# First batch's low rank in two column groups, and the load queue in written order

## The chip, the cores and the metric

The kernel runs on one core of a Trainium2 chip. The metric is the device time of one execution in microseconds, the median over several runs. All stage times below are from one profiled execution of the kernel, counted from the start of its span.

The engines are named as the profile names them: PE is TensorE (PEld its weight loads), DVE is VectorE, ACT is ScalarE, POOL is GpSimd, and SP is SyncE, whose queue issues all the loads and stores of this kernel.

## The reference, cut to what matters

There are 4 batches, 8 heads, a sequence of 768 and a head dimension of 48. A gated recurrence is followed by a mixer with a low-rank mix along the sequence and two dense layers:

```python
f = 1.0 / (1.0 + np.exp(-f_logit))
for t in range(S):
    state = f[:, :, t, :, None] * state + np.einsum('bhd,bhe->bhde', k[:, :, t], v[:, :, t])
    y[:, :, t] = np.einsum('bhd,bhde->bhe', q[:, :, t], state)
x = y.transpose(0, 2, 1, 3).reshape(B, S, H * D)       # (4, 768, 384)
xt = x.transpose(0, 2, 1)
h = xt @ U @ V                                         # U (768, 32), V (32, 768)
u = x + h.transpose(0, 2, 1)
ch = np.maximum(u @ w_ch1, 0.0) @ w_ch2                # (384, 1536), (1536, 384)
return u + ch
```

All of it is 32-bit floating point inside the kernel; the mixer's weights arrive as 64-bit floats.

## The kernel before, in words

**Units.** The recurrence is done for two heads at a time. Such a pair is a *unit*, and a batch has four (`HP`), so there are 16. Unit n loads f, k and q into one of two sets of buffers (`late` for even n, `other` for odd) and v into `v_nat`. `front(n, ...)` makes the gates (`fz`), their running products (scans on DVE) and the scaled keys and queries. `rear(n, ...)` makes the chunk states (`kept`, `states`, `scan`), the scores (`scores`, with the masked product `A` on DVE), and the output in two parts that add up in one PSUM tile `y`: `read` (queries by states) and `inner` (`A` by v). `inner` ends with ACT's copy of `y` into the unit's 96 of the 384 columns of the batch's `x`. After `read`, ACT makes a tiny copy named `seen`.

**The mixer of a batch.** `low_rank` multiplies U by the six row blocks of x into four groups of 32 rows (`ph`), ACT copies the result to `h`; `added_up` adds the four groups with the matrix `blocks` (again `ph` and `h`); `mix` multiplies by V (`pu`) and DVE adds the result to x. `turn` transposes two row blocks of x (`put`), and ACT copies them to `uT`. `ch1` makes the first dense layer from `uT` and w1 (`pz`: six matmuls a call), and ACT evicts it with a ReLU to `z_all` or `zw`. `ch2` makes the second one (`po`). `pz` and `po` share a PSUM pool of two buffers; `pt`, `put`, `pu`, `y` and others share another of three.

**Weights.** `weight_loader` gives each piece of a weight a `start` (the DMA of the 64-bit words into a raw buffer) and an `end`: two passes on ACT (L90, L91), three on DVE (L92 to L94) and one on POOL (L95). The pieces are U, two of V, twelve column blocks of w1 (128 columns each, numbered 0 to 11 here) and twelve row blocks of w2. The first six blocks of w1 are loaded into halves of the buffers of `zw`, which are free until then; the others into `w_raw`, which has four buffers. `ahead_by` starts a load some pieces before the end of an earlier one.

**Order.** PE's order is written out by hand everywhere, that of DVE and ACT in the first batch's attention and what follows it up to `start_mixer(1, ...)`. SP's order is left to a scheduler. `busy(n)` issues n matmuls of no use (`idle`). The first batch's four units run alone, with little else for PE. Then its mixer starts: low rank, sum, part of x, transposes, with two single `busy` calls between, and then the `pz` groups, beside which the next batch's units are worked from the fourth `pz` on (`EARLY`).

**Loads.** The scheduler puts the loads of units 2 and 3, U, V and blocks 0 and 1 of w1, unit 4, most of unit 5, blocks 2 and 3, the v of unit 5, blocks 4 and 5, and then blocks 6 to 9 in SP's queue, in this order.

Of the kernel before, what the change touches and what calls it, by code (L numbers as in the profile page):

```python
# [10 lines left out]
F32 = mybir.dt.float32  # L11
U32 = mybir.dt.uint32
U64 = mybir.dt.uint64
I32 = mybir.dt.int32
AF = mybir.ActivationFunctionType
ALU = mybir.AluOpType
AX = mybir.AxisListType

WP = 384

RAW = 4
# [80 lines left out]
def ahead_by(n, loads):  # L102


    def call(i):
        if i + n < len(loads):
            loads[i + n][0]()
        loads[i][1]()

    return [lambda i=i: call(i) for i in range(len(loads))]  # L110
# [36 lines left out]
class Mixer:  # L147
# [6 lines left out]
    def __init__(self, tc, b, x, U, V, w1, w2, sums, ident, blocks, out, two, three, zp, ps_big, ps_mm, wide=False,  # L154
                 z_all=None, room=None, pair=0):
        nc = tc.nc
        P = nc.NUM_PARTITIONS
        NCH, DM = x.shape[1], x.shape[2]
        R, FF = U.shape[2], w1.shape[2]
        NG = P // R  # L160
        NDC, NFC = DM // P, FF // P
# [3 lines left out]
        uT, z, h, S = {}, {}, {}, {}  # L165

        def low_rank():
            pm = ps_mm.tile([P, 512], F32, name="ph", tag="mm")

            for c in range(NCH):  # L170
                g = slice((c % NG) * R, (c % NG + 1) * R)
                nc.tensor.matmul(pm[g, 0:DM], lhsT=U[:, c, :], rhs=x[:, c, :],  # L172
                                 start=(c < NG), stop=(c >= NCH - NG))
            h[0] = two.tile([P, DM], F32, name="h", bufs=1)
            nc.scalar.copy(h[0], pm[:, 0:DM])

        def added_up():

            pm = ps_mm.tile([P, 512], F32, name="ph", tag="mm")
            nc.tensor.matmul(pm[:, 0:DM], lhsT=blocks, rhs=h[0], start=True, stop=True)  # L180
            h[1] = two.tile([P, DM], F32, name="h", bufs=1)
            nc.scalar.copy(h[1], pm[:, 0:DM])

        def add(*args):

            with tc.high_priority(offset=AHEAD):
                nc.vector.tensor_tensor(*args)  # L187

        pu = {}

        def mix(t):

            s = t % 2
            if s == 0:
                pu[0] = ps_big.tile([P, 2, 512], F32, name="pu", tag="big")
            g = slice((t % NG) * R, (t % NG + 1) * R)
            nc.tensor.matmul(pu[0][:, s, 0:DM], lhsT=V[g, t // NG, :], rhs=h[1][g, :], start=True, stop=True)  # L197
            if s == 1:
                add(x[:, t - 1 : t + 1, :], x[:, t - 1 : t + 1, :], pu[0][:, :, 0:DM], ALU.add)

        def turn(a):

# [231 lines left out]
def factored_path(ctx, tc, q, k, v, f_logit, moe_U, moe_V, moe_w_ch1, moe_w_ch2, out, ok):  # L434
# [4 lines left out]
    nc = tc.nc  # L439
    B, H, S, D = q.shape  # L440
    P = nc.NUM_PARTITIONS
    C = P // 2
    NCH = S // C

    NBL = S // P
    HP = H // 2
    DM = H * D
    R = moe_U.shape[1]
    FF = moe_w_ch1.shape[1]
    NDC = DM // P  # L450
    NFC = FF // P
# [15 lines left out]
    two = ctx.enter_context(tc.tile_pool(name="two", bufs=2))  # L467
    three = ctx.enter_context(tc.tile_pool(name="three", bufs=3))
    zp = ctx.enter_context(tc.tile_pool(name="zp", bufs=3))
    ps_big = ctx.enter_context(tc.tile_pool(name="ps_big", bufs=3, space=bass.MemoryType.PSUM))  # L470
# [20 lines left out]
    def load(n, *names):  # L491

        b, hp = divmod(n, HP)
        for nm in names:
            if nm == "v":
                v_tiles[n] = three.tile([P, NBL, 2, D], F32, name="v_nat")
            for par in range(2):
                head = src[nm][b, 2 * hp + par]
                if nm == "v" and par:

                    for s in range(2):
                        nc.sync.dma_start(
                            out=v_tiles[n][(1 - s) * C : (2 - s) * C, :, par, :],
                            in_=head.rearrange("(c s p) d -> s p c d", s=2, p=C)[s],
                        )
                    continue
                if nm == "v" or n < TURNED:
                    dst = v_tiles[n] if nm == "v" else nat[n % 2][nm]
                    nc.sync.dma_start(out=dst[:, :, par, 0:D], in_=head.rearrange("(c p) d -> p c d", p=P))
                    continue  # L510
                head = head.rearrange("(c i) d -> i c d", i=NB)
                for part in range(2):
                    p0 = par * PAD + part * NB
                    n_ch = min(NB, D - part * NB)
                    nc.sync.dma_start(
                        out=raw[n % 2][nm][p0 : p0 + NB, :].rearrange("p (c d) -> p c d", d=NB)[:, :, 0:n_ch],
                        in_=head[:, :, part * NB : part * NB + n_ch],
                    )
# [9 lines left out]
    blocks = const.tile([P, P], F32, name="blocks")  # L528
# [33 lines left out]
    table = one.tile([P, 1], F32, name="table")  # L562
# [4 lines left out]
    U = const.tile([P, NBL, R], F32, name="U")  # L567
    V = const.tile([P, (NBL * R + P - 1) // P, P], F32, name="V")
    take_in = weight_loader(nc, two, nc.sync)
    weights = [take_in(U, moe_U.rearrange("(c p) r -> p c r", p=P))]  # L570
    weights += [take_in(*pair) for pair in by_rows(V, moe_V, R)]
    early = len(weights)
    w1_rows = moe_w_ch1.rearrange("(c p) f -> p c f", p=P)

    spare = []

    def place():
        if not spare:
            t = zp.tile([P, NFC // 2, 2 * P], F32, name="zw").rearrange("p i t -> p (i t)").bitcast(U64)
            spare.extend([t[:, 0:WP], t[:, WP : 2 * WP]])  # L580
        return spare.pop(0)

    FIRST = 6
    weights += [
        take_in(w1[:, :, i * P : (i + 1) * P], w1_rows[:, :, i * P : (i + 1) * P], place if i < FIRST else None)
        for i in range(NFC)
# [96 lines left out]
    def mixer(b):  # L683
        return Mixer(tc, b, x_tiles[b], U, V, w1, w2, sums if b else None, ident, blocks, out, two, three, zp, ps_big, ps_mm,
                     b == 0, z_all, room if b >= B - 2 else None, FEWER - (b - B + 2) * NCH // 4)
# [172 lines left out]
    def front(n, *names):  # L858

        if n >= NU:  # L860
            return []
        if n not in ahead:
            ahead[n] = dict(zip(("gates", "keep", "keys", "read_back", "queries"), prepare(n)))
        return [ahead[n].pop(nm) for nm in names]

    def rear(n, *names):

        if not 0 <= n < NU:
            return []
        if n not in here:  # L870
            here[n] = dict(zip(("kept", "states", "scan", "scores", "read", "inner"), attend(n)))
        return [here[n].pop(nm) for nm in names if nm in here[n]]
# [43 lines left out]
    with tc.manual_schedule(engines={nc.vector.engine, nc.scalar.engine}):  # L916


        idle = ps_mm.tile([P, 512], F32, name="idle", tag="mm")

        def busy(n):
            for _ in range(n):
                nc.tensor.matmul(idle[:, 0:DM], lhsT=ident, rhs=ends[:, 0:DM], start=True, stop=True)  # L923

        busy(1)
        for piece in front(0, "gates"):
            piece()
        for n in range(HP):
            pieces = front(n, "keep", "keys") + rear(n - 1, "scan", "scores")
            pieces += [lambda: busy(3)] + rear(n, "kept") + front(n, "read_back", "queries")  # L930
            if n + 1 < HP:
                pieces += front(n + 1, "gates") + rear(n - 1, "read", "inner") + rear(n, "states")
            else:
                pieces += rear(n, "states") + rear(n - 1, "read") + rear(n, "scan", "scores") + rear(n - 1, "inner")
            for piece in pieces:
                piece()
            if n < 2:
                load(n + 2, "v")
            if n == 1:


                for start, _ in weights[: early + 2]:
                    start()
            elif n > 1:
                load(n + 2, "f", "k", "q", "v")
        for start, _ in weights[early + 2 : early + FIRST]:
            start()
        loads = ahead_by(early + FIRST, weights)
        for piece in rear(HP - 1, "read") + loads[:2] + rear(HP - 1, "inner") + loads[2 : early + 1]:
            piece()  # L950
        loads = loads[early + 1 :]

        m = mixer(0)
        start = m.before[:5] + m.firsts[0:1] + m.before[5:]
        idles = {1: 1, 2: 1}

        EARLY = 9
        second = chain(front(HP, "gates", "keep", "keys", "read_back", "queries"), steps(HP, 2 * HP + 1))
        for i, (_, piece) in enumerate(start + m.firsts[1:]):
            busy(idles.get(i, 0))  # L960
            piece()
            if loads and i != 1:
                loads.pop(0)()
            if i >= EARLY:
                next(second)()
        for f in loads:
            f()
        n = len(m.seconds) // (NBL // 2)
        todo, after = m.seconds[:-n], m.seconds[-n:]

        attention(second, 12 + 10 * HP - (len(start) + len(m.firsts) - 1 - EARLY), todo)
        m = start_mixer(1, after)
        for f in to_sum:
            f()
# [380 lines left out]
```

## Time and profile before

| What | Value |
|---|---|
| Median of 14 runs | 490.84 us (487.68 to 492.75) |
| The profiled execution: its own time | 491.83 us |
| The profiled execution: its span | 490.1 us |
| Mean granted TensorE clock in it | 0.986 of full |
| Busy: PE, DVE, ACT, POOL | 472.8, 356.2, 163.6, 36.3 us |
| First `ph` matmul of the first batch | 49.18 us |
| First `pz` matmul | 58.61 us |
| Bytes moved by DMA | 34.34 MB |

A line of the timeline gives the start in us, the length in us, the engine, the line of the kernel and operation, the output and input tile, shapes, and the number of records; in brackets the idle time of the engine ahead of it and what ended it. One matmul of 32-bit floats leaves two records on PE. "issue" is time in which the engine waited for nothing that the profile shows. The line of 40 digits named PEclk gives the granted TensorE clock in tenths for each fortieth of the span. For SP the timeline shows when a DMA is issued, not when it lands.

### The profile page before, as it was taken

The page shows a single profiled execution, that of the slowest core. Times are in us where ns is not written, and L with a number is a line of the kernel's source. Part 1 is how long each engine was busy: PE and PEld are TensorE (multiplying, and loading weights), DVE is VectorE, ACT ScalarE, POOL GpSimd, SP SyncE. Part 2 cuts the span into 40 slices and gives each one's busy share as a digit, 9 for nine tenths or more (in the row PEclk, how much of TensorE's full clock was granted, in tenths as well). Part 3 has the DMA queues.
Part 4 walks back from the last instruction along what each step waited for, and adds up shares of the span by engine and source line. Part 5 has one row for each costly group of instructions (what it writes and reads, how often), then busy time and mean ns, then how long its engine had stood idle before and what let it go on. Part 6 is the DMA issues. An engine that isn't in the chain of part 4 may idle for free.

```text
span 490.1 us, 12681 instructions
## 1 busy us (share of the span) xinstructions
PE 472.8 (96%) x5519; PEld 402.1 (82%) x5519; DVE 356.2 (73%) x561; ACT 163.6 (33%) x307; POOL 36.3 (7%) x49
## 2 busy tenths in 40 slices
PE   7897999999999999999999999998999999999995
PEld 4676588886666568899899888898979999999995
DVE  5877798788998847656857548796896796948642
ACT  3343575654334313423231403433131312112200
POOL 3000245452000000000000000000000000000000
PEclk9998899999999999999999999999999999999998
DMA  9989967675678513333435100100000000000001
GB/s 145 158 160 166 243 177 177 159 145 67 107 109 132 83 44 39 49 50 73 68 47 94 32 17 17 27 3 19 19 2 0 34 2 16 17 1 33 0 34 38
DMA packets 158679, 34.34 MB, mean 70 GB/s; under 512 B 149206, under 2 KB 157078, under 8 KB 158614
## 3 DMA queue, kind: packets, MB, share of 16 engines
q1 hardware_dynamic: 158614, 33.44, 37.5%
q8 instruction: 45, 0.74, 0.7%
q14 instruction: 20, 0.16, 0.1%
HBM read 28.70 MB, written 4.72 MB: 68 GB/s over the span
## 4 chain that ended last, share of the span: by engine, by line
PE 91%; DVE 4%; issue 1%; ACT 1%; DMA 1%; SPq 0%; DVEq 0%; ACTq 0%
PE pw L273 26%; PE pz L219 23%; PE pp L371 11%; PE po L244 10%; PE y L842 3%; PE y L824 3%; PE ds L786 3%; PE sc L749 3%; PE pt L621 2%; PE idle L923 2%; PE put L207 2%; PE pt L770 2%; PE pu L197 1%; PE ph L172 1%; DMA late<-in_k_dram 1%
## 5 line engine op out<-in xcount | busy, mean ns | idle before, releaser
L219 PE MATMUL pz<-uT,w 128*128 128x256 f32 x504 | 115.8, 384 | 0.1
L219 PEld LDWEIGHTS pz<-uT,w 128*128 128x128 f32 x504 | 93.3, 190 | 13.3 <-issue 0.3
L273 PE MATMUL pw<-w,z_all 128*128 128x192 f32 x216 | 37.7, 329 | 0.0
L273 PE MATMUL pw<-zw,w_raw 128*128 128x192 f32 x216 | 37.4, 327 | 0.0
L273 PEld LDWEIGHTS pw<-zw,w_raw 128*128 128x128 f32 x216 | 35.2, 190 | 0.8 <-issue 0.6
L273 PEld LDWEIGHTS pw<-w,z_all 128*128 128x128 f32 x216 | 35.0, 190 | 0.7
L655 DVE TENSOR_TENSOR_SCAN late<-fz,late 128x768 f32<-128x768 f32 x16 | 28.1, 1756 | 10.2 <-ACT fz L650 5.1
L95 POOL TENSOR_TENSOR w<-w_y,w_r 128x384 int32<-128x384 int32 x24 | 30.2, 1257 | 36.5 <-DVE w_y L94 29.5
L229 ACT ACTIVATE z_all<-pz 128x512 f32<-128x512 f32 x33 | 19.6, 595 | 39.5 <-PE pz L219 39.4
L371 PE MATMUL pp<-v_nat,late 128*128 128x128 f32 x224 | 28.8, 275 | 0.0
L673 DVE TENSOR_TENSOR_SCAN late<-fz,other 128x768 f32<-128x768 f32 x16 | 27.9, 1745 | 0.1
L371 PEld LDWEIGHTS pp<-v_nat,late 128*128 128x128 f32 x224 | 27.0, 192 | 0.0
L244 PE MATMUL po<-w,zw 128*128 128x384 f32 x72 | 25.6, 499 | 0.0
L244 PE MATMUL po<-w,z_all 128*128 128x384 f32 x72 | 25.3, 496 | 0.0
L364 ACT ACTIVATE other<-other 128x512 f32<-128x512 f32 x18 | 11.3, 631 | 40.0 <-DVE other L187 40.0
L812 ACT COPY st<-added 128x576 f32<-128x576 f32 x12 | 14.7, 1227 | 26.0 <-DVE added L807 26.0
L756 DVE TENSOR_TENSOR A<-sc,causal 128x768 f32<-128x768 f32 x16 | 15.2, 948 | 10.0 <-PE sc L749 10.0
L92 DVE TENSOR_SCALAR w_y<-w_y 128x384 f32<-128x384 f32 (+3 forms) x27 | 11.8, 438 | 12.0 <-ACT w_y L90 11.8
L244 PEld LDWEIGHTS po<-w,zw 128*128 128x128 f32 x72 | 12.9, 189 | 8.7 <-issue 1.2
L244 PEld LDWEIGHTS po<-w,z_all 128*128 128x128 f32 x72 | 13.1, 190 | 8.5 <-DVE o L187 0.6
L842 PEld LDWEIGHTS y<-v_nat,A 64*64 64x64 f32 x768 | 14.1, 145 | 7.1 <-issue 5.4
L187 DVE TENSOR_TENSOR w_raw<-z_all 128x768 f32<-128x768 f32 x12 | 11.5, 954 | 10.5 <-ACT z_all L229 9.2
(185 smaller groups left out, 837.6 us busy)
## 6 DMA issues: line engine op xcount, KB each, us to landing
w_raw<-in_moe_w_ch_dram SPq DMA_DIRECT2D x18, 384.0 KB, 4.0
out_dram<-o SPq DMA_DIRECT2D x24, 192.0 KB, 1.9
v_nat<-in_v_dram SPq DMA_DIRECT2D x16, 144.0 KB, 3.0
v_nat<-in_v_dram SPq DMA_DIRECT2D x32, 72.0 KB, 2.8
zw<-in_moe_w_ch_dram SPq DMA_DIRECT2D x6, 384.0 KB, 6.1
late<-in_f_logit_dram SPq DMA_DIRECT2D x10, 96.0 KB, 3.3
late<-in_k_dram SPq DMA_DIRECT2D x10, 96.0 KB, 2.7
late<-in_q_dram SPq DMA_DIRECT2D x10, 96.0 KB, 2.8
```

What stands on the lines that cost most here:

```text
L95: nc.gpsimd.tensor_tensor(dst.bitcast(I32), shaped(y.bitcast(I32)), shaped(r), ALU.add)
L219: nc.tensor.matmul(pm[:, i * 2 * P : (i + 1) * 2 * P], lhsT=w1[:, m, o : o + P], rhs=uT[a][:, m, :], start=(m == 0), stop=(m == NDC - 1))
L229: nc.scalar.activation(z[a, c][:, k : k + 2, :].rearrange("p i t -> p (i t)"), pm, AF.Relu)
L244: nc.tensor.matmul(pm, lhsT=z[a, i // NI][:, i % NI, s * P : (s + 1) * P], rhs=w2[:, i, :], start=(i == 0), stop=(i == NFC - 1))
L273: nc.tensor.matmul(pm[:, n * HM : (n + 1) * HM], lhsT=lhs[:, i, :], rhs=rhs[:, i, :], start=(i == 0), stop=(i == NI - 1))
L371: nc.tensor.matmul(pm[:, i, r * P : (r + 1) * P], lhsT=room["w"](wn)[:, r * P : (r + 1) * P], rhs=x_node(a, xn), start=((xn, wn) == of[0]) ...
L655: nc.vector.tensor_tensor_scan(backwards(X, S - 1, S), backwards(f, S, S), backwards(ends, S - 1, S), 0.0, ALU.mult, ALU.add,)
L673: nc.vector.tensor_tensor_scan(Y, f[:, 0:S], starts, 0.0, ALU.mult, ALU.add)
L749: nc.tensor.matmul(sc[part[s ^ par], par, c * C : (c + 1) * C], lhsT=T["k"][rows[par], chunk[2 * c + s]], rhs=T["q"][rows[par], chunk[2 * ...
L756: nc.vector.tensor_tensor(T["A"], sc[:, :, 0 : NBL * C].rearrange("p h (c i) -> p h c i", i=C), causal.unsqueeze(1).unsqueeze(1).broadcast ...
L786: nc.tensor.matmul(ds[par * PAD : (par + 1) * PAD, s, c * D : (c + 1) * D], lhsT=T["kb"][part[s ^ par], par, i, :], rhs=vt[part[s ^ par], ...
L842: nc.tensor.matmul(o(s, par, c), lhsT=T["A"][part[s ^ par], par, c, :], rhs=vt[part[s ^ par], c, par, :], start=False, stop=True, skip_gro ...
```

## The change

The first batch's low rank, sum and part of x are done in two groups of columns: the 288 columns of the first three units (`done`), and the 96 of the last (`rest`). The low rank of `done` stands between `read` and `inner` of the last unit, and `mix_of` packs the 96 columns of two row blocks into one PSUM half. The new pieces take their PSUM from the pool of three; the `idle` matmuls between the old pieces are gone. U's and V's conversions stand earlier, between the pieces of the last two units.

SP now follows the written order up to the end of the first batch's attention. Blocks 0 and 1 are followed by blocks 2 and 3, unit 4, blocks 4 and 5, unit 5, and blocks 6 to 9. A column of the raw buffer of block 2 (`held`) is set to zero at the start, and ACT copies it to `table` just after the copy of the first low rank; the load of block 2 overwrites that column, and so waits for this copy. The buffers of `zw` for the six blocks are taken in advance. `EARLY` keeps the fourth `pz` as the place from which the second batch's units are worked.

```diff
+        def low_rank_of(cols):
+            pm = ps_big.tile([P, 2, 512], F32, name="ph", tag="big")[:, 0]
+            for c in range(NCH):
+                g = slice((c % NG) * R, (c % NG + 1) * R)
+                nc.tensor.matmul(pm[g, cols], lhsT=U[:, c, :], rhs=x[:, c, cols],
+                                 start=(c < NG), stop=(c >= NCH - NG))
...
+            nc.scalar.copy(hs[0][:, cols], pm[:, cols])
+
+        def added_up_of(cols):
+            pm = ps_big.tile([P, 2, 512], F32, name="ph", tag="big")[:, 0]
+            nc.tensor.matmul(pm[:, cols], lhsT=blocks, rhs=hs[0][:, cols], start=True, stop=True)
+            nc.scalar.copy(hs[1][:, cols], pm[:, cols])
+
+        def mix_of(cols):
...
+                for k in range(m):
+                    for s in range(2):
+                        i = blocks_of[s][k]
+                        g = slice((i % NG) * R, (i % NG + 1) * R)
+                        nc.tensor.matmul(pm[:, s, k, :], lhsT=V[g, i // NG, :], rhs=hs[1][g, cols], start=True, stop=True)
...
+                add(xv, xv, pm, ALU.add)
...
+    FIRST = 6
+    for _ in range(FIRST // 2):
+        t = zp.tile([P, NFC // 2, 2 * P], F32, name="zw").rearrange("p i t -> p (i t)")
+        spare.extend([t[:, 0 : 2 * WP], t[:, 2 * WP : 4 * WP]])
+    held = spare[2][:, 0:1]
+    nc.gpsimd.memset(held, 0.0)
...
-        busy(1)
...
+        with tc.manual_schedule(engines={nc.vector.engine, nc.scalar.engine, nc.sync.engine}):
+            busy(1)
...
+            pieces = rear(n, "states") + rear(n - 1, "read") + rear(n, "scan") + ends_of[:1] + rear(n, "scores")
+            pieces += ends_of[1:2] + rear(n - 1, "inner") + rear(n, "read") + ends_of[2 : early + 1]
             for piece in pieces:
                 piece()
-            if n < 2:
-                load(n + 2, "v")
-            if n == 1:
+            m = mixer(0)
+            low_rank_of, added_up_of, mix_of = m.some
+            low_rank_of(done)
...
+            nc.scalar.copy(table, held)
+            for i in range(2):
+                for start, _ in weights[early + 2 * i + 2 : early + 2 * i + 4]:
                     start()
-            elif n > 1:
-                load(n + 2, "f", "k", "q", "v")
-        for start, _ in weights[early + 2 : early + FIRST]:
-            start()
-        loads = ahead_by(early + FIRST, weights)
...
+                load(HP + i, "f", "k", "q", "v")
+            for start, _ in weights[early + FIRST : early + FIRST + RAW]:
+                start()
+            ends_of[early + 1]()
+            for piece in rear(HP - 1, "inner"):
+                piece()
+            added_up_of(done)
+            low_rank_of(rest)
+            mix_of(done)
+            added_up_of(rest)
+            mix_of(rest)
+            loads = ahead_by(FIRST - 2 + RAW, weights[early + 2 :])
...
-        m = mixer(0)
-        start = m.before[:5] + m.firsts[0:1] + m.before[5:]
-        idles = {1: 1, 2: 1}
+        start = m.before[3:5] + m.firsts[0:1] + m.before[5:]
-        EARLY = 9
+        EARLY = 6
```

## The prediction

> **What bounds the kernel now.** The page's busy table comes first, then the 40 slices.
>
> ```profile
> PE 472.8 (96%) x5519; PEld 402.1 (82%) x5519; DVE 356.2 (73%) x561; ACT 163.6 (33%) x307; POOL 36.3 (7%) x49
> ...
> PEclk9998899999999999999999999999999999999998
> GB/s 145 158 160 166 243 177 177 159 145 67 107 109 132 83 44 39 49 50 73 68 47 94 32 17 17 27 3 19 19 2 0 34 2 16 17 1 33 0 34 38
> ```
>
> PE (TensorE) sets the time. From 58 us it is full, with 1.7 us of waits up to 350 us (the waits of PE). So the change is worth what it does to the moment from which PE runs full, provided nothing makes PE wait afterwards. I then read PE in order of time:
>
> ```profile
> 45.11 0.25 PE L842 MATMUL y<-v_nat,A 64*64 64x48 f32 x1 [0.26 <-ACT seen L831]
> 46.82 1.52 PE L842 MATMUL y<-v_nat,A 64*64 64x48 f32 x47 [1.45 <-issue]
> 49.18 2.78 PE L172 MATMUL ph<-x,U 128*32 128x384 f32 x12 [0.84 <-ACT x L848]
> 51.89 1.60 PE L923 MATMUL idle<-late,ident 128*128 128x384 f32 x2
> ...
> 56.75 1.74 PE L207 MATMUL put<-ident,x 128*128 128x128 f32 x12 [0.40 <-DVE x L187]
> 58.61 2.83 PE L219 MATMUL pz<-uT,w 128*128 128x256 f32 x12
> 61.27 0.82 PE L207 MATMUL put<-ident,x 128*128 128x128 f32 x6
> 61.93 8.07 PE L219 MATMUL pz<-uT,w 128*128 128x256 f32 x36
> 69.84 0.82 PE L621 MATMUL pt<-ident,late 128*128 128x128 f32 x6
> 70.49 5.34 PE L219 MATMUL pz<-uT,w 128*128 128x256 f32 x24
> ```
>
> A serial bridge runs from 49 to 58.6: low rank, sum, part of x, transposes, with idle matmuls as padding. Twelve records are one group of six matmuls (pz: 2.7 us). I call the groups pz0, pz1 and so on: pz4 starts at 70.49. The loads and their conversions are the other stream:
>
> ```profile
> 33.04 0.95 SPq L81 DMA_DIRECT2D zw<-in_moe_w_ch_dram  x2
> 34.04 2.63 SPq L509 DMA_DIRECT2D late<-in_f_logit_dram  x2
> ...
> 53.89 1.68 SPq L81 DMA_DIRECT2D zw<-in_moe_w_ch_dram  x2
> 55.61 2.48 SPq L81 DMA_DIRECT2D w_raw<-in_moe_w_ch_dram  x4
> ```
>
> ```profile
> 64.76 0.56 ACT L90 ACTIVATE w_y<-w_raw 128x384 f32<-128x384 f32 x1 [0.26 <-POOL w L95]
> 65.23 0.56 ACT L91 ACTIVATE w_r<-w_raw 128x384 int32<-128x384 uint32 x1
> 65.68 0.59 ACT L229 ACTIVATE z_all<-pz 128x512 f32<-128x512 f32 x1
> ```
>
> w1 comes in twelve column blocks; two are issued at 33.04, then two units' loads, and block 6 (the first w_raw) at 55.61. ACT converts block 6 at 64.76, about when it evicts pz1: the conversions sit between PSUM evictions in ACT's order.
>
> [...] granted 0.50 from 47 to 53 us, after gaps of 0.43, 0.26 and 1.45 us, though a gap of 1.41 at 330.8 did not trip it. [...] The instruction queue moved 45 packets, 0.74 MB, so 16 KB each; from the gap at 42.00 to that at 45.36 there are 127 matmul records, each with its weight load[...]. [...]
>
> **The change, part by part. (1) The bridge.** The rows of three units (288 columns) are reduced before the last unit's inner products; four idle records (1.60 + 0.81 us) go.
> - U's conversion moves up on ACT to 42.0, behind the first "seen". Its three DVE steps (0.26 + 0.26 + 0.36) follow the scan that ends at 42.87 and push A 0.9 us back, to 44.8, still before its use. POOL (0.59) has U ready at 44.5.
> - The last read ends at 44.4 to 44.9. [...] With SP silent from 34 to 47 I take 1.5 us off: low rank starts at 45.3 (kept gap: 46.8).
> - Low rank at full clock took 1.48 us for 384 columns (at 164.7 us), so 1.1 for 288, to 46.4. ACT still owes conversions of the last V piece and block 0, whose buffer waits for POOL, so its copy ends at 47.6 and the copy to `table` at **T0 = 47.8**.
> - Inner products 0.9, to 47.3. ACT converts block 1 (1.0) ahead of the eviction of x (0.64): x at 49.4, against 49.04 before.
> - Small low rank 0.6, to 50.0; the part of 288 on PE to 51.1; three DVE adds of 0.72 (0.96 for 768 scaled to 576 elements) from 50.4 to 52.6; the sum of 96 waits for the buffer freed by add 1, the part of 96 for that by add 2; add 4 (0.5) ends at 53.1. Transposes at 53.1, and 1.86 later, as now, pz0 at **55.0 against 58.61: 3.6 us gained**.
>
> **(2) The loads.** Block 2 goes into a buffer that ACT's copy to `table` reads first, so SP stops there until T0, and behind it wait, in written order: block 3, unit 4 (nine DMAs), blocks 4 and 5, unit 5 (nine), blocks 6 to 9. Formerly both units had nearly left by then.
> - A block is 0.39 MB, a unit 1.18 MB. To land block 6: five blocks, 1.97 MB, at 347 GB/s (58 to 62 us) = 5.7 us; two units, 2.36 MB, at 164 GB/s (4.3 to 14 us) to 200 (42 to 44 us) = 14.4 to 11.8; about 2 for start and landing (a lone U of 192 KB took 3.0). Sum 19.5 to 22.1; at the mean of 212 GB/s from 34 to 62 us it is 22.4. I take 21.5: block 6 at **69.3**; block 4 (three blocks 3.4, a unit 7, and 2) at T0 + 12.5 = 60.3.
> - ACT's new order is: eviction 0, block 4, uT2, block 5, eviction 1, block 6, eviction 2. So pz2 (needs uT2) waits: 60.3 + 1.0 + 0.8 = 62.1, where PE could start it at 61.0. pz3 ends near 67.5. pz4 needs the buffer of pz2 (two in its pool), so eviction 2, so block 6: 69.3 + 1.0 + 0.6 = **71.0 against 70.49: 0.5 us lost** where 3.6 were gained. With the bounds of T0 and the rates it lies between 1.5 gained and 1.8 lost.
> - Queued behind ACT's wait: evictions, uT2 and the sigmoid of unit 4; behind these DVE's scan. Blocks 6 to 9 take DVE 1.95 us each, end to end, ahead of that scan; ACT's copy of `least` waits for it before an eviction. Estimated 0.3 (0 to 1).
>
> **(3) The clock.** PE idles some 1 us before pz2 and, after the 0.7 us of unit 4's transposes, 2.8 us before pz4: more than the 1.45 that tripped it. [...] I take 1.7.
>
> **(4) At nothing.** The memset on POOL (one column) and the extra ACT copy lie in waits. Extra `h` buffers add no wait. w2's last conversion falls behind the last pz; its use is several groups later. PE's order after pz0 is the old one, so a shift at pz4 goes through to the end.
>
> **Sum:** +0.5 + 0.3 + 1.7 = **+2.5 us**. On the profiled execution (span 490.1, time 491.83, 1.0 above the median) that is 494.3; on the median of 490.84, **493.3**.
>
> **Rivals.**
> - *Forecast: late loads and a clock loss* (0.62): 491.9 to 497, ending slower.
> - *The start is kept* (0.20), the other side: the queue packs better than I think, the blocks land before ACT reaches them, pz4 goes with PE. For: 347 GB/s is seen when blocks run alone, and SP no longer stops for buffers. Against: units never beat 200 to 240. To keep all of 3.6 block 6 must land by 65.3, 281 GB/s from T0, giving 487.2. It decides at 68.8: earlier landings gain, if the clock holds. A moderate case keeps 1.5: 489.3.
> - *A draw* (0.18): block 6 at 68 to 69.5[...]: about 490.8.
> - *Everything late*: rate 200 GB/s or less, T0 at 49[...]: block 6 at 72, so +3.2 + 3.4, 497.4. It is the far end of the first case.
> - *The hold doesn't hold*: only if the loads needn't wait for the copy to `table`. The code writes what that copy reads; I give it nothing of its own.
>
> **How the numbers follow.** A measurement of this kernel can tell about 0.2%, 1.0 us, from no change. Slower by more: the first case, 0.62. Within: 0.18. Faster: 0.20. The range leaves out the full gain and the double mishap: 488.2 to 497.0; the likeliest case's own is 491.9 to 497.
>
> **What would show it.** Right: pz0 near 55; SP silent from 34 to about 48; ACT's L90 waiting for DMA on zw and w_raw between 58 and 70; PE waiting for ACT before the transposed uT2 and before pz4; PEclk at 0.5 near 71. Wrong: pz4 before 69, no wait of ACT on a weight DMA, or block 6 landing under 19 us after the copy to `table`; also a pz0 later than 57, which would fault part (1).

## The result, and the profile after

| | Before | After |
|---|---|---|
| Median | 490.50 us (47 runs, 487.68 to 494.92) | 494.36 us (10 runs, 492.15 to 496.57) |
| The profiled execution: its own time | 491.83 us | 492.69 us |
| Its span | 490.1 us | 491.0 us |
| Mean granted clock in it | 0.986 | 0.994 |
| First `pz` matmul (pz0) | 58.61 us | 53.01 us |
| pz4 | 70.49 us | 70.65 us |

The ratio of after to before is 1.0078, with a 95% interval of 1.0059 to 1.0097: the change makes the kernel slower by 3.9 us.

Two accidents separate the two profiled executions, and they must be taken out before the traces are compared. The first is a stretch at half clock at 22 to 26 us, which before had and after had not. The windows view of before shows it (stretch, length, busy time of PE, PEld, DVE, ACT and POOL with the number of records, granted clock, DMA share, GB/s), and PE's timeline where it had reached the third unit's inner products:

```profile
22.00:24.00 2.00, 1.74 (x68) 1.55 (x63) 1.89 (x2) 0.28 (x3) 0.00 (x0) 0.65 0.90 156
24.00:26.00 2.00, 2.00 (x59) 1.91 (x53) 0.29 (x3) 1.07 (x2) 0.00 (x0) 0.50 0.42 77
```

```profile
42.95 0.90 PE L842 MATMUL y<-v_nat,A 64*64 64x48 f32 x48
```

After reaches these inner products at 40.71, 2.2 us earlier. Of this, 1.7 us stand already at the second unit's (31.23 against 32.92). They are taken for an accident: e8 below, a variant of the changed kernel, has the same stretch, the other variants have not, and before's traced execution is 1.3 us above its median. The other 0.5 us fall where before waited 0.43 us on "issue" and after did not, and may be the change's own. The second accident is a gap of 1.41 us at 330.8 that only before had. Below, "relative" means counted from the third unit's inner products.

PE's timeline of after, by start, length, operation, and in brackets the idle time and what ended it:

```profile
40.71 0.90 PE L886 MATMUL y<-v_nat,A 64*64 64x48 f32 x48
...
43.62 1.16 PE L208 MATMUL ph<-x,U 128*32 128x288 f32 x11 [0.19 <-issue]
...
53.01 4.02 PE L258 MATMUL pz<-uT,w 128*128 128x256 f32 x12
...
61.42 5.45 PE L258 MATMUL pz<-uT,w 128*128 128x256 f32 x24 [1.14 <-ACT uT L247]
...
70.65 5.45 PE L258 MATMUL pz<-uT,w 128*128 128x256 f32 x24 [3.13 <-ACT z_all L268]
```

From the inner products to pz0 it is 12.30 us, where before took 15.66 (42.95 to 58.61). So the bridge did get 3.4 us shorter. (Before also ran much of its bridge at half clock, from 46 to 54 us, and after did not before pz0; e5 below shows how much of the gain that can be.) From pz0 to pz4 it is 17.64, where before took 11.88. Three things are in the difference of 5.8: pz0 at half clock (4.02 instead of 2.83), a wait of 1.14 for `uT`, and a wait of 3.13 for the eviction to `z_all`. All that the bridge had gained is gone at pz4, and 2.4 us more.

What made ACT late is in its own timeline (same columns):

```profile
45.42 0.20 ACT L999 COPY table<-zw 128x1 f32<-128x1 f32 x1
...
59.69 0.55 ACT L90 ACTIVATE w_y<-zw 128x384 f32<-128x384 f32 x1 [2.03 <-DMA zw<-in_moe_w_ch_dram]
60.59 0.78 ACT L247 COPY uT<-put 128x768 f32<-128x768 f32 x1
...
62.16 0.59 ACT L268 ACTIVATE z_all<-pz 128x512 f32<-128x512 f32 x1
69.12 0.55 ACT L90 ACTIVATE w_y<-w_raw 128x384 f32<-128x384 f32 x1 [6.37 <-DMA w_raw<-in_moe_w_ch_dram]
70.01 0.58 ACT L268 ACTIVATE z_all<-pz 128x512 f32<-128x512 f32 x1
```

ACT stands 2.03 us for block 4, and `uT` for pz2 is copied behind it. It stands 6.37 us for block 6, and the eviction that pz4 needs is behind that. Neither the copy nor the eviction needs the block. They are only behind it in order.

And what made the blocks late is in SP's timeline, whose lines tell when a DMA is issued:

```profile
32.40 14.30 SPq L81 DMA_DIRECT2D zw<-in_moe_w_ch_dram  x4
46.74 1.07 SPq L548 DMA_DIRECT2D late<-in_f_logit_dram  x2
...
54.58 2.27 SPq L81 DMA_DIRECT2D zw<-in_moe_w_ch_dram  x2
56.89 1.08 SPq L548 DMA_DIRECT2D other<-in_f_logit_dram  x2
...
65.29 6.21 SPq L81 DMA_DIRECT2D w_raw<-in_moe_w_ch_dram  x5
```

The 14.30 us of the first line are four blocks with the hold between the second and the third: the waits of SP show 11.3 us in a single wait for `table` (L999). Then the queue alternates: blocks 2 and 3, unit 4 (46.74 to 54.5), blocks 4 and 5, unit 5 (56.89 to 64.8), block 6 at 65.29. The queue moves data in every microsecond from 47 to 76 us (123 to 362 GB/s), and every unit in it stands ahead of blocks that are needed sooner.

### The profile page after: what moved, and what is told of

It is laid out like the page before. It is cut to its first block, busy times and chain, and to the rows that moved or that the text cites. A ratio compares the mean times of both kernels' runs of the same rounds, so it can differ in the third digit from the quotient of the medians.

```text
span 491.0 us, 12736 instructions
## 1 busy us (share of the span) xinstructions
PE 471.2 (96%) x5541; PEld 401.1 (82%) x5541; DVE 357.1 (73%) x563; ACT 162.9 (33%) x310; POOL 37.6 (8%) x50
## 4 chain that ended last, share of the span: by engine, by line
PE 68%; DVE 15%; DMA 6%; SPq 5%; issue 3%; ACT 3%; POOL 0%; DVEq 0%; ACTq 0%
PE pw L312 25%; PE pz L258 16%; PE pp L410 11%; SPq L548 2%; DVE late L699 2%; PE y L868 2%; PE ds L830 2%; PE y L886 2%; DVE late L717 2%; PE po L283 2%; PE pt L665 2%; PE sc L793 2%; PE idle L967 2%; DMA late<-in_f_logit_dram 1%; DVE w_y L94 1%
## 5 line engine op out<-in xcount | busy, mean ns | idle before, releaser
L258 PE MATMUL pz<-uT,w 128*128 128x256 f32 x504 | 117.5, 387 | 4.9 <-ACT z_all L268 3.7
L95 POOL TENSOR_TENSOR w<-w_y,w_r 128x384 int32<-128x384 int32 x24 | 31.4, 1306 | 46.9 <-DVE w_y L94 39.4
L92 DVE TENSOR_SCALAR w_y<-w_y 128x384 f32<-128x384 f32 (+3 forms) x27 | 15.1, 559 | 18.3 <-ACT w_y L90 18.0
L403 ACT ACTIVATE other<-other 128x512 f32<-128x512 f32 x18 | 11.3, 631 | 39.9 <-DVE other L187 39.9
L312 PE MATMUL pw<-w,other 128*128 128x192 f32 x108 | 18.6, 327 | 0.0
```

Of the source, the lines that this page charges most:

```text
L92: nc.vector.tensor_scalar(f, f, SMALLEST, LARGEST, ALU.max, ALU.min)
L95: nc.gpsimd.tensor_tensor(dst.bitcast(I32), shaped(y.bitcast(I32)), shaped(r), ALU.add)
L258: nc.tensor.matmul(pm[:, i * 2 * P : (i + 1) * 2 * P], lhsT=w1[:, m, o : o + P], rhs=uT[a][:, m, :], start=(m == 0), stop=(m == NDC - 1))
L312: nc.tensor.matmul(pm[:, n * HM : (n + 1) * HM], lhsT=lhs[:, i, :], rhs=rhs[:, i, :], start=(i == 0), stop=(i == NI - 1))
```

## The experiments

Theory: the bridge is worth about 3.5 us, the hold makes the queue start late, and what loses the time is that the two units stand ahead of blocks 4 to 9. Rivals: the hold itself is the loss; the bridge brings nothing, and only the half clock and the waits on issue move; the loss is the last weight conversion in front of the second batch's scan. The twelve kernels were timed beside before in three groups, in which before had medians of 490.51 (e1 to e4), 490.83 (e5 to e8) and 490.62 (e9 to e12).

| Kernel | Median, us (runs) | Ratio to before, 95% interval |
|---|---|---|
| e1 no hold | 489.94 (22) | 0.9989 (0.9973 to 1.0004) |
| e2 blocks first | 486.43 (6) | 0.992 (0.990 to 0.9941) |
| e3 hold later | 497.92 (6) | 1.0148 (1.0126 to 1.0171) |
| e4 last conversion earlier | 493.79 (8) | 1.0062 (1.0032 to 1.0092) |
| e5 e2 with the old bridge | 490.77 (14) | 0.9994 (0.9974 to 1.0014) |
| e6 e2 without the hold | 491.54 (22) | 1.0015 (1.0002 to 1.0028) |
| e7 e2 with all conversions a group earlier | 492.23 (22) | 1.0028 (1.0011 to 1.0045) |
| e8 hold earlier | 490.00 (14) | 0.9986 (0.997 to 1.0002) |
| e9 e7 with unit 5 later | 486.75 (6) | 0.9923 (0.9903 to 0.9943) |
| e10 e2 with unit 5 later | 487.29 (9) | 0.993 (0.9901 to 0.996) |
| e11 e2 again | 487.16 (6) | 0.9928 (0.9908 to 0.9949) |
| e12 e9 with two idle matmuls | 486.36 (9) | 0.9929 (0.9905 to 0.9952) |

### e1: the change without the hold

```diff
-    nc.gpsimd.memset(held, 0.0)
...
-            nc.scalar.copy(table, held)
```

> The changed kernel without the hold: no memset of the held column and no copy to the table, so block 2 and all behind it leave SP's queue right after block 1, in the same written order. Theory (late loads cost, the new bridge gains): block 6 lands near 60 us, ACT never waits on a weight, PE's waits of 1.1, 3.1 and 0.6 us between 60 and 80 us go, and the kernel is 2 to 3.5 us faster than before (487 to 488.5). Rival (the silent queue is what makes the bridge short[...]): [...]the clock falls to half, the first pz starts 2 to 4 us later, and the kernel is within 1 us of before.

Measured: 489.94, as before within the spread, and 4.4 under after. ACT waits for no weight DMA in its profile, so the theory was right that the hold makes the blocks late. But it forecast a gain over before, and there is none. PE's timeline of e1:

```profile
43.41 0.74 PE L792 MATMUL sc<-qT,kz 48*64 48x64 f32 x34 [3.13 <-issue]
...
47.86 2.13 PE L208 MATMUL ph<-x,U 128*32 128x288 f32 x11 [1.30 <-issue]
...
58.40 2.83 PE L258 MATMUL pz<-uT,w 128*128 128x256 f32 x12 [0.33 <-ACT uT L247]
```

PE waits 3.13 and 1.30 us for nothing that the profile shows, in the middle of a row of matmuls of one kind, runs the low rank at half clock (2.13 instead of 1.16), and pz0 starts at 58.40: about where before has it, whose 58.61 includes the 1.7 us of its early stretch at half clock. In after the one such gap in this place is 0.19. So the rival holds. A good part of what the new bridge wins is won by the silent load queue (at most 12 GB/s in after from 40 to 46 us, 94 to 209 in e1 from 40 to 48), and the hold is what silences it.

### e2: the blocks ahead of the units, hold kept

```diff
             nc.scalar.copy(table, held)
+            for start, _ in weights[early + 2 : early + FIRST + RAW]:
+                start()
             for i in range(2):
-                for start, _ in weights[early + 2 * i + 2 : early + 2 * i + 4]:
-                    start()
                 load(HP + i, "f", "k", "q", "v")
-            for start, _ in weights[early + FIRST : early + FIRST + RAW]:
-                start()
```

> The changed kernel with the hold, but behind it first blocks 2 to 9 of w1 and then units 4 and 5. Theory (what costs is that two units of 1.18 MB stand ahead of the blocks that ACT converts between evictions): block 6 lands about 8 us after the copy to the table instead of 23.5, so ACT waits for no weight and pz4 starts with PE, some 4 us earlier than in the changed kernel; 488 to 490, 1 to 3 us faster than before. Rival (any load behind the hold is too late): unit 4's f then lands late instead, and PE waits ahead of its transposes near 66 us; 492 or more.

Measured: 486.43, below the 488 to 490 of its theory, 4.1 under before and 7.9 under after. The edit changes nothing but the order of 26 loads. In PE's timeline the waits before pz2 and pz4 are gone, and pz0 is where after has it:

```profile
53.19 2.83 PE L258 MATMUL pz<-uT,w 128*128 128x256 f32 x12 [0.33 <-ACT uT L247]
...
64.93 5.34 PE L258 MATMUL pz<-uT,w 128*128 128x256 f32 x24
```

Why the order matters so much is seen in the DMA view of two stretches of e2. In the first only blocks move, in the second only units:

```profile
DMA packets 2069, 2.04 MB, mean 340 GB/s; under 512 B 80, under 2 KB 2069, under 8 KB 2069
```

```profile
DMA packets 5426, 1.03 MB, mean 171 GB/s; under 512 B 5425, under 2 KB 5425, under 8 KB 5425
```

From 48 to 54 us packets of 986 bytes on average (2.04 MB by 2069) moved at 340 GB/s, from 62 to 68 us packets of 190 bytes at 171 GB/s, and the packets' time was 103% and 114% of what sixteen engines have, so the engines were full in both. By these rates a unit of 1.18 MB takes about as long as 2.36 MB of weights, six blocks (an estimate). Put first, the eight blocks delay the last issue of unit 4 by 8.1 us (from 54.5 to 62.7) and that of unit 5 by 4.5 (from 64.8 to 69.3), and PE waits for neither. Put first, the two units delay the issue of block 6 by 17.4 (from 47.92 to 65.29).

Not all of the 7.9 us is waiting. The trace of e2 has no half clock, and the mean granted clock of its six executions is 0.998, against 0.992 for the twelve executions of after whose clock is known. At a like clock (0.996) there are two executions of each: 487.19 and 487.81 of e2, 492.15 and 493.35 of after. So some 5 us remain when the clock is the same.

### e3: the hold later by about 4 us

```diff
-            nc.scalar.copy(table, held)
-            for i in range(2):
...
             added_up_of(rest)
+            nc.scalar.copy(table, held)
+            for i in range(2):
...
```

The copy and all the loads behind it stand after the sum of the last 96 columns, in the change's order.

> The changed kernel with the copy to the table, and so the hold's end, put behind the last copy of h (4.3 us later in the profile of the changed kernel). Theory (the time from the hold's end to block 6 sets pz4): pz4 and the kernel's time go up one for one, by 3.5 to 4.5 us, to 498 to 499. Rival (the loss comes from elsewhere, from the clock or the order on ACT and DVE, and the loads are hidden): less than 1.5 us on top of the changed kernel.

Measured: 497.92, 3.6 over after. PE's timeline of e3 has the same bridge (pz0 at 53.56) and longer waits:

```profile
66.66 7.41 PE L258 MATMUL pz<-uT,w 128*128 128x256 f32 x24 [7.02 <-ACT uT L247]
...
76.52 5.45 PE L258 MATMUL pz<-uT,w 128*128 128x256 f32 x24 [1.79 <-ACT z_all L268]
```

The hold ends at 50.55 instead of 45.62, which relative to the third unit's inner products is 4.2 us later, and the median grows by 3.6. The late queue is on the path. That this is nearly one for one isn't shown by e3 alone: in its trace the 24 records of pz2 and pz3 run partly at half clock (7.41 us instead of 5.45), so some of the 3.6 can be clock.

### e4: the last conversion one group earlier

```diff
-            if loads:
-                loads.pop(0)()
+            for _ in range(2 if i == 12 else 1):
+                if loads:
+                    loads.pop(0)()
```

> The changed kernel with two conversions instead of one after one pz in the middle, so that none is left behind the last pz. Theory (the last conversion stands on DVE ahead of unit 6's scan, and the late scan makes ACT's small copy late, for which PE waited 0.29 and 0.63 us near 123 and 135 us): 0.8 to 1.4 us faster than the changed kernel, 493.0 to 493.6. Rival (these waits come from the general lag): no difference beyond 0.4 us.

Measured: 493.79, 0.6 under after and within the spread of both: inconclusive as a time. In the trace the theory holds: the waits of PE for `seen` fell from 1.7 us to 0.8 (three, of at most 0.3), the two near 123 and 135 us are gone, and the distance to before grows by 0.4 us from 98 to 180 us, where that of after grows by 1.3. The profile shows something else too. The part before pz4 is unchanged in the code, and this execution lost the clock there. PE's timeline, and the windows view in the columns given above:

```profile
71.82 8.43 PE L258 MATMUL pz<-uT,w 128*128 128x256 f32 x24 [3.33 <-ACT z_all L268]
```

```profile
70.00:72.00 2.00, 0.18 (x1) 0.18 (x2) 1.06 (x3) 1.70 (x4) 0.00 (x0) 0.77 0.97 307
72.00:74.00 2.00, 2.00 (x5) 1.64 (x6) 1.91 (x4) 1.64 (x5) 1.09 (x1) 0.50 0.62 163
74.00:76.00 2.00, 2.00 (x6) 1.55 (x6) 1.93 (x4) 1.24 (x4) 1.00 (x1) 0.50 0.93 245
76.00:78.00 2.00, 2.00 (x7) 1.58 (x6) 0.22 (x1) 0.66 (x2) 0.99 (x1) 0.53 0.73 197
```

The same 24 records took 5.45 us in after, at full clock. So the wait of 3.13 in after and of 3.33 in e4 cost 3.0 us more in one execution than in the other. What the four stretches lack of full clock adds up to 3.4 us.

### e5: e2 with the old bridge

```diff
-            low_rank_of(done)
+            for piece in rear(HP - 1, "inner"):
+                piece()
+            whole = slice(0, DM)
+            low_rank_of(whole)
             nc.scalar.copy(table, held)
...
+            busy(1)
+            added_up_of(whole)
+            busy(1)
+            mix_of(whole)
```

> The order of e2 (hold, then blocks 2 to 9, then units 4 and 5), but with the bridge of the kernel before: the last unit's inner products first, then low rank, sum and part of x over all 384 columns, with the two idle matmuls; the hold ends behind the copy of that low rank. Theory A (the two column groups shorten the bridge by 3.4 us, as the prediction summed): 3 to 3.5 us slower than e2, 489.5 to 490. Theory B (most of the earlier first pz comes from a silent queue[...] and the column groups add little): at most 1.5 us slower than e2, 486.5 to 488.

Measured: 490.77, 4.3 over e2 and a little beyond theory A. PE's timeline of e5:

```profile
44.66 0.93 PE L886 MATMUL y<-v_nat,A 64*64 64x48 f32 x47 [1.04 <-issue]
...
56.61 2.83 PE L258 MATMUL pz<-uT,w 128*128 128x256 f32 x12
```

pz0 falls from 53.19 to 56.61, by 3.4 us. More is lost behind it, because in this bridge the hold ends 4.0 us later (49.80 against 45.80): ACT waits 3.23 us for block 10, and PE 0.55 us for an eviction at 80.75 and 0.29 for one at 103.16. The trace also has half clock from 45 to 53 us, which e2 has not, but the clock is not the whole difference: the one execution of e5 with a mean clock of 1.000 took 489.87, the two of e2 486.19 and 486.52. The bridge in two column groups is worth 3 to 4 us once the loads let it through, and blocks first with a hold alone is worth nothing against before.

### e6: e2 without the hold

```diff
-    nc.gpsimd.memset(held, 0.0)
...
-            nc.scalar.copy(table, held)
```

> The order of e2 (blocks 2 to 9, then units 4 and 5) without the hold, so SP issues it all from 33 us on. Theory [...]: waits on issue of 1 to 3 us between 40 and 48 us as in e1, the clock at half, 3 to 4 us slower than e2, 489.5 to 490.5. Rival [...]: within 1 us of e2, 485.5 to 487.5.

Measured: 491.54, 5.1 over e2: the theory's waits and half clock, and more loss than it forecast. PE's timeline of e6:

```profile
43.56 1.23 PE L792 MATMUL sc<-qT,kz 48*64 48x64 f32 x34 [2.82 <-issue]
```

The gap falls on the same matmuls as in e1 (34 records before the end of the last unit's scores), with a different order of loads; pz0 follows at 57.92. What e1 and e6 have in common, and after and e2 have not, is a queue that moves data at that moment. The windows view, e6 first and then e2:

```profile
40.00:42.00 2.00, 0.74 (x34) 0.60 (x27) 1.71 (x3) 1.33 (x6) 0.00 (x0) 1.00 1.09 361
```

```profile
40.00:42.00 2.00, 1.97 (x119) 1.83 (x116) 1.93 (x4) 1.14 (x6) 0.00 (x0) 1.00 0.04 8
```

At 361 GB/s PE is busy for 0.74 us of these two, at 8 GB/s for 1.97; in e2 the same matmuls show no gap. Before had its gap at the same matmul, but of 0.43 us only, with 149 GB/s moving from 41 to 42.4 us, and e5, e7, e8 and e9 waited 0.16 to 0.44 there in the silence. So at this place the long waits are seen only where the queue moves data, but a moving queue doesn't always bring one.

### e7: e2 with all remaining conversions one group earlier

```diff
-            if loads:
-                loads.pop(0)()
+            for _ in range(2 if i == 1 else 1):
+                if loads:
+                    loads.pop(0)()
```

> e2 with two conversions instead of one after the second transposes, as far ahead as in the kernel before, so that none is left behind the last pz. Theory (PE's waits of 0.44 and 0.63 us for the small copy near 117 and 129 us come from that last conversion): both go, 0.8 to 1.2 us faster than e2, 485.2 to 485.7. Rival (the waits come from the place of unit 6's loads or from ACT): no difference beyond 0.4 us.

Measured: 492.23. Theory and rival both missed. ACT's timeline of e7 shows a wait that neither had:

```profile
74.40 0.55 ACT L90 ACTIVATE w_y<-w_raw 128x384 f32<-128x384 f32 x1 [4.15 <-DMA w_raw<-in_moe_w_ch_dram]
```

Conversions a group earlier also need block 10 a group earlier, and in SP's queue block 10 stands behind unit 5. It is after's fault again, one buffer cycle later: ACT waits 4.15 us, DVE's scan and ACT's `least` follow, and PE waits 3.34 us before a `pz` group.

### e8: the change with the hold released earlier

```diff
-            pieces = rear(n, "states") + rear(n - 1, "read") + rear(n, "scan") + ends_of[:1] + rear(n, "scores")
+            pieces = rear(n, "states") + rear(n - 1, "read") + rear(n, "scan") + ends_of[:1]
+            pieces += [lambda: nc.scalar.copy(table, held)] + rear(n, "scores")
...
-            nc.scalar.copy(table, held)
```

> The changed kernel with its own load order, but the copy to the table stands right behind U's first conversions on ACT, some 4.7 us earlier. Theory (pz4 follows the hold's end one for one until PE itself bounds it near 66 us[...]): block 6 lands near 64.5, pz4 starts at 66 to 67, 3 to 4 us faster than the changed kernel, 490.3 to 491.5. Rival [...]: a wait on issue of over 1 us there, half clock, and at most 2 us faster than the changed kernel.

Measured: 490.00, 4.4 under after, a little more than the theory gave. The traced execution had the half clock at 22 to 26 us that before had, so it is read relative to the third unit's inner products, the first of these lines of PE:

```profile
44.27 0.90 PE L886 MATMUL y<-v_nat,A 64*64 64x48 f32 x48
...
48.16 1.16 PE L208 MATMUL ph<-x,U 128*32 128x288 f32 x11 [1.56 <-issue]
...
57.15 2.83 PE L258 MATMUL pz<-uT,w 128*128 128x256 f32 x12 [0.33 <-ACT uT L247]
...
69.76 5.45 PE L258 MATMUL pz<-uT,w 128*128 128x256 f32 x24 [0.70 <-ACT z_all L268]
```

Counted so, the hold ends 5.1 us earlier than in after, and pz4 comes after 25.49 us instead of 29.94. Block 6 is still late (ACT waits 4.4 us for it), but PE waits only 0.70 before pz4. The rival's gap is there, 1.56 us in the first low rank, but at full clock it makes the bridge only 0.6 us longer (12.88 instead of 12.30). With e3 this shows the late queue from both sides: an end of the hold 4.2 us later cost 3.6, one 5.1 us earlier brought 4.4. Over 3 us are then left against e2; e8 keeps the change's order of the loads.

### e9, e10, e11, e12: what is left in e2

e11 is e2 without a change. e10 and e9 issue unit 5's loads behind the third piece of the mixer's loop, with SP in written order up to there; e9 has e7's extra conversion besides, and e12 adds two matmuls to e9:

```diff
-            for i in range(2):
-                load(HP + i, "f", "k", "q", "v")
+            load(HP, "f", "k", "q", "v")
...
+                if i == 2:
+                    load(HP + 1, "f", "k", "q", "v")
```

```diff
+            nc.tensor.matmul(idle[:, 0:P], lhsT=ident, rhs=ends[:, 0:P], start=True, stop=True)
             added_up_of(rest)
+            nc.tensor.matmul(idle[:, 0:P], lhsT=ident, rhs=ends[:, 0:P], start=True, stop=True)
             mix_of(rest)
```

What was expected of e11:

> The same kernel as e2 once more, on this chip and beside these runs. If blocks ahead of units is what turns the change's loss into a gain, it is again 3 to 5 us faster than before: ratio 0.990 to 0.994. [...]

Of e10:

> As e9 without the extra conversion: unit 5's loads issued behind the third piece of the loop. Theory (unit 5 is not needed until far later and block 10's wait of 1.5 us on ACT in e2 was covered): within 0.7 us of e2, 485.8 to 487, with ACT's wait for block 10 gone and PE's waits for `seen` as in e2 (about 1.1 us together). Rival (that wait on ACT does reach PE): 0.8 us or more faster than e2.

Of e9:

> As e2 (blocks 2 to 9 first, then units 4 and 5), with unit 5's loads issued behind the third piece of the mixer's loop and two conversions at the second piece, so that blocks 10 and 11 leave SP ahead of unit 5 and all conversions are done one group earlier. Theory (what is left of the loss is the last conversion in front of DVE's scan, and the two-conversion variant of e7 failed only because block 10 stood behind unit 5): ACT waits under 0.5 us for block 10, PE's waits for `seen` fall under 0.4 us together, time 485 to 486. Rival (the extra conversion delays `least` or an eviction wherever it stands, or unit 5's later loads now end last): a wait of over 1 us on PE before a pz group or at unit 5, time 487.5 or more.

Of e12:

> As e9, with one idle matmul of 128 columns before the sum and one before the part of x of the last 96 columns, to hold the clock over the short gaps of the bridge. Theory (those gaps cost nothing where the clock is already full, and the matmuls lie in gaps): within 0.5 us of e9. Rival 1 (the half clock at the first pz group in some executions comes from these gaps): 0.5 to 1.5 us faster than e9. Rival 2 (they lengthen the bridge): 0.3 to 0.8 us slower.

Measured: e11 487.16, so e2's lead is there again (486.43 and 487.16 against 490.5 and 490.6). e10 487.29: as forecast, ACT's waits for weights are gone and the time is e2's, so those waits were covered. e9 486.75: against e7 it confirms why e7 failed (the wait of 4.15 us for block 10 is gone, ACT's only wait for a weight is 1.19 us for a later one at 82.91, no `pz` group waits for `z_all`, and the time falls by 5.5 us), but its own theory, 485 to 486, missed. The waits of PE show why, e11's first and then e9's (total us, times, longest us):

```profile
PE y L886 <- ACT seen L875: 1.7, 5, 0.6
PE pz L258 <- ACT uT L247: 0.3, 1, 0.3
```

```profile
PE pz L258 <- ACT uT L247: 0.9, 1, 0.9
PE y L886 <- ACT seen L875: 0.8, 3, 0.3
```

The extra conversion takes 0.9 us off the waits for `seen` and puts 0.9 on pz2, because it now stands ahead of the copy of `uT` on ACT. e12 486.36: 0.4 under e9, inside the spread of both, so no gain in time is shown for the idle matmuls. The granted clocks do differ: eight of e12's nine executions have a mean of 0.997 or more, e9's six 0.991 to 0.996, and the trace of e12 has no half clock up to 480 us where that of e9 has it from 50 to 54 us. The idle matmuls seem to hold the clock in the bridge, as rival 1 supposed. e2, e9, e10, e11 and e12 can't be told apart; they are 3.3 to 4.3 us faster than before and beat both kernels.

## Why the prediction came out

The forecast was 493.3, slower; measured 494.36. The direction came out for the reason given, late loads; that the size is so near is in part luck, as the sum below shows. The steps:

- **(1) The bridge: right.** 3.6 us gained was forecast, 3.4 is measured relative to the third unit's inner products (the absolute 53.0 against 55.0 is mostly before's stretch at half clock). e5 against e2 gives 3.4 at pz0 and 4.3 in time. The 1.5 us that it took off the wait on issue "with SP silent", an estimate of the author's, turned out to be the hinge: e1 and e6 lose the bridge without that silence, with waits of 3.13 and 2.82 us. The prediction listed this as one term of a sum and didn't see that the hold, which costs the loads their start, is also what pays for the bridge.
- **(2) The loads: right in mechanism, too small.** Silence of SP, L90 waiting on `zw` and `w_raw`, pz2 behind `uT2` and pz4 behind the third eviction all came as written. The copy to `table` ended at 45.6, which with the shift of 2.2 is the forecast 47.8. Block 6 was forecast 21.5 us after it, 19.5 to 22.4 at the outside; ACT took it after 23.5 (45.62 to 69.12), and in e3, e4 and e8 after 24.1 to 24.5. The mis-sized term is the two units: at 164 to 200 GB/s (the windows named show 164 and 195) they were to take 11.8 to 14.4 us together, and their issues took 7.8 and 7.9. So pz4 came out 2.4 us late relative to before, not 0.5. That block 6 (69.12 against 69.3) and pz4 (70.65 against 71.0) still fall where they were forecast in the trace's own time is luck: this execution was 2.2 us early, and the loads were 2.0 slow.
- **`least`: 0.3 forecast.** PE waits 0.61 for an eviction at 79.95, behind ACT's wait of 3.31 for `least`; from pz4 to 82 us the distance to before grows by 1.0. That is the upper bound that was given.
- **(3) The clock: 1.7 forecast, not in after's profile, and no net loss against before.** PE waited 3.13 us before pz4 and kept full clock. In e4 3.33 us cost 3.0, nearer to the 3.4 us of full clock that before lacked at 46 to 54 us than to the 1.7 that it lacked at 22 to 26. The 1.7 of the forecast was the author's estimate. Why the clock dropped after the one wait and not after the other isn't shown. The half clock that after's profile does have, at pz0, was not in the sum, and was covered there: pz2 had to wait for `uT` anyway (in e4, with pz0 at full clock, it waited 2.98 us instead of 1.14). How many of after's executions lose the clock at pz4 is open, since only one is traced. But every execution has its mean granted clock: 0.992 on average for the twelve of after, and 0.992 for the 105 of before beside the experiments. So the medians are not 3.9 us apart because after loses more clock than before.
- **(4) "At nothing": wrong for w2's last conversion.** "Its use is several groups later" looks at who uses the weight. What counts is what stands behind it on DVE. In before the scan of unit 6 starts at 117.99; in after the conversion is between (DVE's timeline):

```profile
119.66 0.36 DVE L92 TENSOR_SCALAR w_y<-w_y 128x384 f32<-128x384 f32 x1 [1.45 <-ACT w_y L90]
...
120.93 1.75 DVE L699 TENSOR_TENSOR_SCAN late<-fz,late 128x768 f32<-128x768 f32 x1
```

ACT's `least` waits for that scan, `seen` is behind `least`, and PE's inner products wait for `seen`: 0.29 us at 123.04 and 0.63 at 135.69, where before had no such wait in either place. The distance to before grows by 1.3 us from 98 to 180 us (0.9 of it are these two waits). In e9, where the conversions are a group earlier, it doesn't grow at all there.

The sum of the profile pair: +2.4 up to pz4, +1.0 from there to 98 us, +1.3 to 180, then −1.6 for the gap at 330.8 that only before had, and −2.2 by which before came later to the third unit's inner products: +0.9, as the two times say (492.69 against 491.83). The medians are 3.9 apart, since before's profiled execution was 1.3 above its median and after's 1.7 below. For before the clock explains this: its traced execution had a mean of 0.986 where 0.992 is usual, 3 us of clock less, and a line through its 105 executions rises by 0.5 us for each us of clock lost, so some 1.5 (an estimate). For after it doesn't: 0.994 is only a little above its average. A clock lost at pz4 would be of the right size for that, but is only shown for e4.

So the forecast sum of 2.5 and the measured 3.9 are near each other although their terms are not. Relative to before, 2.4 are lost up to pz4 where 0.5 was forecast, 2.3 more by 180 us, behind waits on ACT and DVE, where 0.3 was forecast, and the 1.7 for the clock is not shown as a net loss.

Of the rivals, "the start is kept" needed block 6 at 65.3 at the latest, 63.1 with the shift; it came at 69.1. "Everything late" is close to what e3 built: 497.9 against the 497.4 forecast for it. Its 3.4 for the clock was an estimate too; the half clock of e3's trace, at 63 to 71 us, lacks as much.

## What to carry to other kernels

When loads of different packet sizes share one queue, order them by what is due first, and count each by its time in the queue and not by its bytes (blocks moved at 340 GB/s in e2, units at 171): here eight blocks in front of two units cost the units up to 8 us that nobody missed, while the two units in front of the blocks cost 7.9 us of the total. For every wait that a change adds on an engine with a fixed order, list what stands behind it and doesn't need it (here a copy of `uT`, an eviction, and a scan); the user of the late data is rarely the first to suffer. A dense row of small matmuls was worth a quiet load queue here (waits of 3.13 and 2.82 us with it moving in e1 and e6, of at most 0.44 with it silent), but the quiet must be paid for with an order that lets the most urgent load go first when it ends.

## What the runs showed of the hardware

- In one place the long waits on "issue" came with a moving load queue. The same row of `sc` matmuls waited 3.13 us (e1) and 2.82 (e6) with SP's queue moving data, and at most 0.44 with it silent. But before waited only 0.43 there with its queue moving, and silence doesn't end such waits: with 6 GB/s moving, an `sc` matmul of before waited 1.41 us at 330.8, and with none an inner product of e5 1.04 us at 43.6. What PE waits for in these gaps isn't shown: the profile says only "issue".
- The length of a gap alone doesn't decide whether the clock drops: 3.13 us left it at full (after, pz4), 3.33 didn't (e4), nor did 2.82 (e6, whose 34 `sc` records then took 1.23 us, against 0.74 in e1). In before, gaps of 0.43, 0.26 and 1.45 us within 5 us were followed by half clock (0.50 from 47 to 53). And four short waits of 0.77, 0.36, 0.33 and 0.36 us between 46 and 52 us were followed by PEclk 0.50 from 52 to 54 (after) but not in e11, with 0.54, 0.36, 0.33 and 0.36.
- What a drop of the clock took here came in two sizes. In windows of 1 us up to 480 us, each stretch below full clock in the fourteen traces lacks either 1.7 us of full clock (before at 22 to 26, after at 52 to 56, e10 at 51 to 55) or 3.4 us (before at 46 to 54, e1 at 45 to 52, e3 at 63 to 71, e4 at 71 to 78). How much of it reached the time differed: the 1.7 of after was covered, since pz2 had to wait for `uT` anyway, and the 3.4 of e4 cost 3.0 us on the same 24 records (8.43 against 5.45).
